# Pooled attention and two feed-forward layers in one kernel: conversions in equal pieces, attention stages at fixed slots, batch 0's value sums issued first

## The chip, the cores and the metric

The kernel runs on one core of a Trainium2 chip. A core has five engines that each work through a queue of their own, in order: PE (matrix products), DVE (elementwise work and reductions), ACT (copies and functions), POOL and SP (here mostly issuers of DMAs). They wait for each other by semaphores. The metric is the time of one execution in microseconds on the device; lower is better.

## The reference, cut to what matters

```python
# q, k, v: (8 batches, 8 heads, 576 positions, 64); keys and values are averaged over groups of 8 positions (72 left)
scores = scale * np.matmul(q, k_p.transpose(0, 1, 3, 2))
attn = softmax(scores)                       # over 72
x = np.matmul(attn, v_p)                     # -> (4608 tokens, 512)
x = (((x @ w1) * (x @ w2)) @ w3) @ w_out     # d_ff 1024
h = x @ w_in                                 # d_ff 2048
out = (softplus(h)) @ w_out2
```

Everything is float32, and the weights of the linear layers arrive as 64-bit words, which the kernel converts.

## The kernel before, in words

**Tiling.** The 4608 tokens are 6 passes (s = 0 to 5) of 768 tokens. Attention works on 36 groups (g) of 128 tokens, six for a pass, one pass ahead of its use. Each float32 product is three fast products of a high and a low part: `split` (L126) makes the parts, a copy on ACT (L128) and a subtraction on DVE (L129); `mm3` (L131) issues the three (L133 to L135). The first layer's `w3 @ w_out` is multiplied into one matrix W beforehand ("the fold", `W_mm`, L552).

**Stages in time.** First the fold, with groups 0 to 2 beside it. Then pass 0 with plain products, 16 `plain_step`s (L685). Then passes 1 to 5, each 8 `one_step`s (L739) of seven products (a Strassen scheme that needs sums of quarters of the weights and of x); their result x2 goes to DRAM. Then the second layer (from L894), 48 steps that reload x2, multiply by `w_in`, apply softplus and multiply by `w_out2`.

**Slots.** Between the products of a step the code calls a slot: four in a plain step, seven in `one_step`. Each slot may issue products of the x2 accumulation (`x2_groups`), one or more stages of attention (`att_slot`, from the table `sched` that `stages` and `begin` fill, L484 to L502), a part of the next pass's x factors (`x_steps`, L656) and a number of steps of background work (`bg`, L214). All of this is written out in program order; nothing is reordered later, so what a slot issues stands in each engine's queue at that place.

**Attention of a group.** `scores` (PE, L405), `maxima` (DVE, L417 and L418), `exps` (ACT, L424, one for each head), `normalize` (DVE, L429 to L431), `p_transpose` (PE L440 and a copy on ACT, L441), `pv` (PE, L456). Keys and values are summed over eight positions by DMAs that accumulate into one buffer (`pool_step`, L369): each waits for the one before on POOL's queue. Batch 0's keys are summed on DVE instead (`pool_k0`, L362), its values by two chains of four DMAs (L377) and one addition on DVE (L380).

**Background.** `next_job` (L199) converts the weights in pieces: `magnitudes` on ACT (L148), then pieces on DVE (L157 and L159, L162, L167), for w12 also a split (L172, L176). After these jobs `left_factors` (L256) runs through the rest of the program: sums of the quarters of w12 (8 tiles), conversion and sums of `w_in` (8 tiles, raw load L265), conversion of `w_out2` (8 tiles, raw load L338, pieces L244 to L251, copies L329, differences L331). Its results go to DRAM from a ring of two staging buffers (`put`, L275: copy L279, difference L281, DMA L285) and come back as weights by `load_factors` on POOL's queue (L637). `load_x2` (L795) reloads x2 for the second layer on SP's queue, first at the end of step 5 of pass 5.

Of the kernel before, what the change touches and what calls it, by code (L numbers as in the profile page):

```python
# [51 lines left out]
def pooled_attention_two_ffn(ctx: ExitStack, tc: tile.TileContext, qT_d, k0_d, kT_d, v_d, w12_d, w3T_d, wo_d, wi_d, wo2_d, out):  # L52
# [98 lines left out]
    def convert_steps(raws, dsts, y, ahead):  # L151
# [11 lines left out]
        yield  # L163
# [5 lines left out]
        if isinstance(dsts[0], tuple):  # L169
            yield  # L170
# [71 lines left out]
    def convert_1024(raw, y):  # L242
        yi = y.bitcast(I32)
        nc.scalar.activation(y, raw[:, :, 1].bitcast(F32), AF.Abs, scale=HI_SCALE)  # L244
        yield
        nc.vector.tensor_scalar(y, y, HI_MIN, HI_MAX, op0=ALU.max, op1=ALU.min)
        nc.vector.tensor_scalar(yi, yi, 3, None, op0=ALU.logical_shift_left)
        yield
        nc.vector.scalar_tensor_tensor(yi, raw[:, :, 1], -0x80000000, yi, op0=ALU.bitwise_and, op1=ALU.bitwise_or)
        yield  # L250
        nc.vector.scalar_tensor_tensor(yi, raw[:, :, 0], 29, yi, op0=ALU.logical_shift_right, op1=ALU.bitwise_or)  # L251
        yield

    sums_made = set()

    def left_factors():  # L256
# [4 lines left out]
        a11, a12, a22, a21 = (y[:, 256 * i:256 * i + 256] for i in range(4))  # L261
# [5 lines left out]
        def sums():  # L267
            nc.vector.tensor_add(s1, a21, a22)
            nc.vector.tensor_sub(s3, a11, a21)
            yield  # L270
            nc.vector.tensor_sub(s2, s1, a11)
            nc.vector.tensor_sub(s4, a12, s2)
            yield

        def put(src, dsts):  # L275
            n = src.shape[1]
            st = stage([P, 2, 512])[:, :, :n]
            hi = st[:, 0, :].bitcast(F32R)
            nc.scalar.activation(hi, src, AF.Copy)  # L279
            yield  # L280
            nc.vector.tensor_sub(st[:, 1, :].bitcast(F32R), src, st[:, 0, :])  # L281
            n //= len(dsts)
            for i, dst in enumerate(dsts):
                dst = dst.rearrange("p h c f -> p h (c f)") if len(dst.shape) == 4 else dst
                nc.sync.dma_start(dst, st[:, :, n * i:n * i + n])  # L285
            yield

        def put_sums(w3_, w4_):
            yield from put(S[:, :512], [w3_[:, :, 2, :], w4_[:, :, 0, :]])
            yield from put(S[:, 512:], [w4_[:, :, 1, :], w4_[:, :, 3, :]])  # L290
# [7 lines left out]
        for t in range(F8):  # L298
            y = ys[t % 2]
            a11, a12, a22, a21 = (y[:, 256 * i:256 * i + 256] for i in range(4))  # L300
            if t + 1 < F8:
                nc.sync.dma_start(ys[(t + 1) % 2], w12y[t + 1])
            yield from sums()
# [704 lines left out]
```

## Time and profile before

| what | value |
|---|---|
| median of 3 runs | 1601.32 us (1600.45 to 1604.28) |
| the profiled execution | 1600.07 us |
| its span on the core | 1598.2 us |
| PE busy | 1507.9 us (94%) |
| DVE, ACT, POOL busy | 1056.2, 838.1, 225.4 us |
| DMA over the span | 311.84 MB, mean 195 GB/s |

The span is the stretch that the trace covers. Rows of the view by windows give, for a stretch of the span in us, each engine's busy time with the number of its instructions in brackets, the mean granted clock of PE (1.00 is 2.4 GHz, 0.50 is 1.2 GHz), the busy share of the DMA engines and what they moved. Rows of the waits name who waited for whose instruction and line, in us over all, the number of waits, and the longest. Rows of a timeline give start, duration, engine, line, operation, output<-input with sizes and the count of merged instructions, and in brackets the engine's idle time just before, with what ended it. Rows of the groups by line give the total and the mean in ns of one. DMA rows give the count, the size of one, and the median from issue to landing in us. Lines are those of the kernel before.

### The profile page before, as it was taken

The numbers are of one execution on the slowest core, as the hardware profiler recorded it, in microseconds if no ns is written. First come the engines' busy times: TensorE is split into PE (matmuls) and PEld (weight loads), VectorE is DVE, ScalarE is ACT, GpSimd is POOL, SyncE is SP. The second block draws the span as 40 slices with busy tenths as digits, with TensorE's granted clock in tenths as the row PEclk, the third lists the DMA queues.
The fourth block names the chain that finished last, engine by engine and source line by source line (L and its number), as shares of the span: only waits on it lengthen the run. The fifth ranks groups of instructions, "written<-read, shape, count | busy, mean of one in ns | idle before, by whom it ended". The sixth has DMA issues, their size and how long they took to land.

```text
span 1598.2 us, 22189 instructions
## 1 busy us (share of the span) xinstructions
PE 1507.9 (94%) x8336; PEld 1363.0 (85%) x8336; DVE 1056.2 (66%) x1678; ACT 838.1 (52%) x1780; POOL 225.4 (14%) x347
## 2 busy tenths in 40 slices
PE   3888998989999999999989999999999999999998
PEld 1458998878999999999879988988898998898897
DVE  5777456557566575576536777777677677768665
ACT  3445545445545555553326466556556556556554
POOL 4311221132213131000101100000000000000000
PEclk9899999999999999999999999999999999999999
DMA  8888796788869787768955635336335334434431
GB/s 262 225 268 237 198 265 186 236 238 260 261 216 279 238 239 246 220 224 301 320 195 191 230 119 192 123 113 209 115 120 183 127 119 152 158 113 134 144 111 40
DMA packets 108011, 311.84 MB, mean 195 GB/s; under 512 B 10853, under 2 KB 49893, under 8 KB 95616
## 3 DMA queue, kind: packets, MB, share of 16 engines
q0 software_dynamic: 41296, 189.03, 39.6%
q1 hardware_dynamic: 66608, 121.39, 22.2%
q8 instruction: 66, 1.08, 0.3%
q14 instruction: 41, 0.34, 0.1%
HBM read 249.56 MB, written 60.82 MB: 194 GB/s over the span
## 4 chain that ended last, share of the span: by engine, by line
PE 78%; DVE 10%; DMA 6%; ACT 4%; issue 2%; POOL 0%; SPq 0%; ACTq 0%; DVEq 0%; POOLq 0%
PE o L875 8%; PE o L874 8%; PE o L873 8%; PE X L133 7%; PE X L134 6%; PE X L135 6%; PE Z L133 5%; PE Z L134 5%; PE Z L135 5%; PE x2p L134 3%; PE x2p L133 3%; PE x2p L135 3%; PE pv L456 2%; PE Wp L555 2%; PE sc L405 2%
## 5 line engine op out<-in xcount | busy, mean ns | idle before, releaser
L133 PE MATMUL X<-area_r 128*128 128x384 f32 x528 | 182.8, 346 | 9.9 <-DVE area_f L768 7.8
L134 PE MATMUL X<-area_r 128*128 128x384 f32 x528 | 178.0, 337 | 0.0
L135 PE MATMUL X<-area_r 128*128 128x384 f32 x528 | 177.8, 337 | 0.0
L128 ACT ACTIVATE area_r<-area_f 128x768 fp32r<-128x768 f32 (+1 forms) x153 | 108.7, 723 | 127.4 <-DVE area_f L775 88.0
L129 DVE TENSOR_TENSOR area_r<-area_f,area_r 128x768 fp32r<-128x768 f32 (+1 forms) x153 | 121.9, 807 | 81.0 <-ACT area_r L128 80.7
L642 POOL DMA_DIRECT2D area_r<-wis x96 | 51.0, 531 | 696.8 <-PE X L135 684.8
L845 ACT ACTIVATE area_f<-area_f 128x768 f32<-128x768 f32 x96 | 81.3, 847 | 126.8 <-DVE area_f L939 125.3
L875 PE MATMUL o<-area_w,area_r 128*128 128x512 f32 x360 | 142.6, 396 | 0.3 <-DVE area_r L129 0.3
L874 PE MATMUL o<-area_w,area_r 128*128 128x512 f32 x360 | 141.9, 394 | 0.0
L873 PE MATMUL o<-area_w,area_r 128*128 128x512 f32 x360 | 140.0, 389 | 0.0
L133 PE MATMUL Z<-area_r 128*128 128x384 f32 x384 | 131.4, 342 | 8.2 <-DVE area_f L759 8.2
L849 DVE TENSOR_SCALAR area_f<-area_f 128x768 f32<-128x768 f32 x96 | 53.8, 561 | 122.0 <-ACT area_f L846 122.0
L134 PE MATMUL Z<-area_r 128*128 128x384 f32 x384 | 129.2, 337 | 0.0
L135 PE MATMUL Z<-area_r 128*128 128x384 f32 x384 | 128.8, 336 | 0.0
L133 PEld LDWEIGHTS X<-area_r 128*128 128x128 f32 x528 | 99.8, 189 | 21.2 <-DVE area_f L768 11.1
L424 ACT ACTIVATE pr<-sc,mx 128x72 f32<-128x72 f32 x288 | 88.5, 330 | 37.4 <-DVE mx L418 36.6
L134 PEld LDWEIGHTS X<-area_r 128*128 128x128 f32 x528 | 99.9, 189 | 3.9
L642 POOL DMA_DIRECT2D area_r<-w12s x80 | 46.9, 587 | 387.9 <-PE X L135 369.9
L135 PEld LDWEIGHTS X<-area_r 128*128 128x128 f32 x528 | 99.7, 189 | 0.0
L855 DVE TENSOR_TENSOR area_f<-area_f 128x768 f32<-128x768 f32 x96 | 92.0, 958 | 6.7 <-ACT area_f L852 0.5
L851 DVE SCALAR_TENSOR_TENSOR area_f<-area_f 128x768 f32<-128x768 f32 x96 | 92.0, 958 | 3.2
L854 DVE SCALAR_TENSOR_TENSOR area_f<-area_f 128x768 f32<-128x768 f32 x96 | 91.4, 952 | 0.0
(166 smaller groups left out, 3895.6 us busy)
## 6 DMA issues: line engine op xcount, KB each, us to landing
area_r<-wis POOLq DMA_DIRECT2D x48, 1024.0 KB, 5.1
area_r<-w12s POOLq DMA_DIRECT2D x40, 1024.0 KB, 6.2
area_r<-wis POOLq DMA_DIRECT2D x48, 768.0 KB, 4.5
area_r<-w12s POOLq DMA_DIRECT2D x40, 768.0 KB, 6.5
area_f<-in_wo_dram SPq DMA_DIRECT2D x24, 512.0 KB, 5.0
wis<-area_f SPq DMA_DIRECT2D x40, 256.0 KB, 5.5
vb<-in_v_dram POOLq DMA_DIRECT2D x64, 144.0 KB, 5.6
xr<-x2d SPq DMA_DIRECT2D x12, 768.0 KB, 7.6
```

The lines of the kernel that those rows point to most:

```text
L128: nc.scalar.activation(hi, src, AF.Copy)
L129: nc.vector.tensor_sub(lo, src, hi.bitcast(F32))
L133: nc.tensor.matmul(ps, whi, xhi, start=first, stop=False, skip_group_check=resumed)
L134: nc.tensor.matmul(ps, whi, xlo, start=False, stop=False, skip_group_check=resumed)
L135: nc.tensor.matmul(ps, wlo, xhi, start=False, stop=last, skip_group_check=resumed)
L642: nc.gpsimd.dma_start(wgroup[n, i], src[i].bitcast(F32R))
L851: nc.vector.scalar_tensor_tensor(e, u, 1.0, e, op0=ALU.subtract, op1=ALU.subtract)
L854: nc.vector.scalar_tensor_tensor(c, c, 0.0, e, op0=ALU.max, op1=ALU.subtract)
L855: nc.vector.tensor_add(c, c, u)
L873: nc.tensor.matmul(oacc[s][i], hl[:, 0, ts], wh, start=first, stop=False)
L874: nc.tensor.matmul(oacc[s][i], hl[:, 0, ts], wl, start=False, stop=False)
L875: nc.tensor.matmul(oacc[s][i], hl[:, 1, ts], wh, start=False, stop=last)
```

## The change

The conversions' generators yield less often, so that one background step holds a piece of work of about equal size: the empty steps are gone, `left_factors` no longer goes through `put` but issues two copies in one step (`highs`) and the two differences with their DMAs in another (`lows`), and `sums` is one step. A job of the fold takes 3 steps instead of 4, a job of w12 4 instead of 6, and `left_factors` 156 instead of 235. The counts of steps in each slot are new. Attention groups begin at other slots, and from group 12 on each group lies at the same seven slots of a step: scores in slot 3, four exps in slot 4 and four in slot 5, normalize in slot 6, the transposition in slot 1 of the next step and pv in its slot 2. Background steps then run in slots 0, 2 and 4 of steps 0 to 5 of passes 1 to 4, in five slots of other steps, and hardly beside the x factors, of which one piece goes into each slot of the last step and the first slots of the next; before pass 1 two go into each of four slots. Batch 0's value sums are issued earlier on POOL's queue. What is computed is the same; only the order of the instructions changes.

```diff
         for i in both:
             nc.vector.scalar_tensor_tensor(yi[i], raws[i][:, :, 1], -0x80000000, yi[i], op0=ALU.bitwise_and, op1=ALU.bitwise_or)
-        yield
         ahead()
         yield
...
         yield
         if isinstance(dsts[0], tuple):
-            yield
             for i in both:
...
-        def put(src, dsts):
-            n = src.shape[1]
-            st = stage([P, 2, 512])[:, :, :n]
-            hi = st[:, 0, :].bitcast(F32R)
-            nc.scalar.activation(hi, src, AF.Copy)
-            yield
-            nc.vector.tensor_sub(st[:, 1, :].bitcast(F32R), src, st[:, 0, :])
...
+        def highs(*srcs):
+            for src in srcs:
+                st = stage([P, 2, 512])[:, :, :src.shape[1]]
+                nc.scalar.activation(st[:, 0, :].bitcast(F32R), src, AF.Copy)
+                staged.append((src, st))
+
+        def lows(*dsts):
+            for to in dsts:
+                src, st = staged.pop(0)
+                nc.vector.tensor_sub(st[:, 1, :].bitcast(F32R), src, st[:, 0, :])
+                n = src.shape[1] // len(to)
+                for i, dst in enumerate(to):
+                    dst = dst.rearrange("p h c f -> p h (c f)") if len(dst.shape) == 4 else dst
+                    nc.sync.dma_start(dst, st[:, :, n * i:n * i + n])
...
         for t in range(F8):
-            yield from convert_1024(raw, y)
+            magnitude()
+            yield
+            shift()
+            yield
+            sign()
+            if t:
+                highs(S[:, :512], S[:, 512:])
+            yield
+            tail_of(t - 1)
+            yield
+            last_bits()
             if t + 1 < F8:
                 load_wi(t + 1)
             else:
                 load_raw_wo2(raw, 0)
-            yield from sums()
+            yield
+            sums(y)
+            yield
+            highs(y[:, :512], y[:, 512:768])
+            yield
             w3_, w4_ = wis[t]
-            yield from put(y[:, :512], [w3_[:, :, 0:2, :]])
-            yield from put(y[:, 512:768], [w4_[:, :, 2, :]])
-            yield from put_sums(w3_, w4_)
+            lows([w3_[:, :, 0:2, :]], [w4_[:, :, 2, :]])
+            yield
...
-    begin = [6 * n for n in range(3)] + [START + 1 + 13 * n // 2 for n in range(9)]
-    begin += [PLAIN + STEADY * s + 1 + 8 * n for s in range(4) for n in range(6)]
+    begin = [6 * n for n in range(3)] + [START + 2 + 19 * n // 3 for n in range(9)]
+    begin += [PLAIN + STEADY * s + 7 * n + 3 for s in range(4) for n in range(6)]
...
-        return [(0, all_[0]), (0, all_[1]), (1, es(0, 1)), (2, es(2, 3, 4)), (3, es(5, 6, 7)), (4, tail[0]), (6, tail[1]), (7, tail[2])]
+        return [(0, all_[0]), (0, all_[1]), (1, es(0, 1, 2, 3)), (2, es(4, 5, 6, 7)), (3, tail[0]), (5, tail[1]), (6, tail[2])]
...
         load_q(0)
+        kv_step()
         make_identity(nc, ident)
...
         for n in range(NJ0):
-            bg(4)
+            bg(3)
             for m in ((0, 1), (2,), (3,), ())[n]:
                 pool_k0(m)
-            if n:
-                kv_step()
+            kv_step()
             W_ready(6)
...
-        for slot in (0, 2, 4):
-            at(slot, kv_step)
+        at(3, kv_step)
         for n in range(START):
             att_slot()
             W_ready(2)
-            bg((1, 2, 2)[n % 3])
+            bg((1, 1, 2)[n % 3])
...
                 att_slot()
-                bg(2 if half == 0 and n < 4 else 1)
+                bg(1)
...
-                if (half, n) == (1, F8 - 1):
+                if (half, n) == (1, F8 - 1) and slot_now[0] > PLAIN - 4:
+                    next(xs)
                     next(xs)
...
+            tile = s < NS - 1 and n < 6
+            steps = (2, 4) if n == 0 else () if n == 7 else (0, 2, 4) if tile else (0, 3, 4, 5, 6)
+
             def slot(k):
-                x2_groups((1, 0, 1, 0, 1, 1, 4)[k])
-                busy = slot_now[0] in heavy
+                x2_groups(((1, 0, 0, 0, 1, 2, 4) if tile else (1, 1, 1, 0, 1, 1, 3))[k])
                 att_slot()
-                if n in (0, F8 - 1) and next(xs_of[s + (n > 0)], True) is None and k % 3:
-                    return
-                if not busy and k != 5:
-                    bg(2 if s == NS - 1 and k in (3, 6) else 1)
+                if n in (0, F8 - 1):
+                    next(xs_of[s + (n > 0)], None)
+                if k in steps:
+                    bg(1)
```

The first place is POOL's queue at the start of the program, before group 0's `pv`. `vb_0`, `vb_1` are the buffers of batch 0's values, `kT` the pooled keys that the scores read. Before:

```order
L358 DMA area_f<-in_k_dram 128x576 x4
L350 DMA q_143<-in_qT_dram 128x512
masks.py:197 MEMSET ident 128x128
masks.py:199 ISA
masks.py:199 AFFINE_SELECT ident<-ident 128x128
L533 MEMSET kT_134 128x576
L533 MEMSET kT_135 128x576
L367 COPY kT_134<-area_e 64x72 x6
L377 DMA vb_0_197<-in_v_dram 72x512
L377 DMA vb_1_198<-in_v_dram 72x512
L367 COPY kT_134<-area_e 64x72 x2
```

The same queue after the change, from its first load of the values:

```order
L405 DMA vb_0_145<-in_v_dram 72x512
L405 DMA vb_1_146<-in_v_dram 72x512
masks.py:197 MEMSET ident 128x128
masks.py:199 ISA
masks.py:199 AFFINE_SELECT ident<-ident 128x128
L561 MEMSET kT_134 128x576
L561 MEMSET kT_135 128x576
L395 COPY kT_134<-area_e 64x72 x4
L405 DMA vb_0_145<-in_v_dram 72x512
L405 DMA vb_1_146<-in_v_dram 72x512
L395 COPY kT_134<-area_e 64x72 x2
L405 DMA vb_0_145<-in_v_dram 72x512
```

The first pair of value loads moved ahead of eight copies and memsets, and the other pairs stand between the copies instead of behind six of them.

The second place is SP's queue at the end of pass 5. `w2s` are the converted tiles of `w_out2` on their way to DRAM, `area_f<-in_wo_dram` a raw load of it, `x2d_69` the x2 of pass 0 that the second layer's first factors are made from. Before:

```order
L338 DMA area_f<-in_wo_dram 128x1024 x2
L332 DMA w2s_121<-area_f 256x1x512 x2
L332 DMA w2s_122<-area_f 256x1x512
L798 DMA xr_127<-x2d_69 128x4x384
L798 DMA xr_128<-x2d_69 128x4x384
L332 DMA w2s_122<-area_f 256x1x512
```

After:

```order
L366 DMA area_f<-in_wo_dram 128x1024 x2
L274 DMA w2s_121<-area_f 256x1x512 x2
L642 DMA x2d_73<-area_e 128x384 x3
L274 DMA w2s_122<-area_f 256x1x512 x2
L642 DMA x2d_73<-area_e 128x384
L826 DMA xr_127<-x2d_69 128x4x384
L826 DMA xr_128<-x2d_69 128x4x384
```

The reload no longer stands between two stores of the last `w_out2` tile; that tile is finished before it, and the last raw load lies further ahead.

The third place is ACT's queue around group 16's transposition in pass 1. L279 and, after the change, L264 are copies into a staging buffer that must have been stored before; L441 and L469 bring the transposed probabilities to `pv`. Before:

```order
L279 ACTIVATE area_f<-area_f 128x512
L424 ACTIVATE pr_2602,sm_2604<-sc_1_2595,mx_2603 128x72 x3
L762 ACTIVATE area_f<-X 128x384
L765 ACTIVATE area_f<-Z 128x384
L279 ACTIVATE area_f<-area_f 128x512
L441 ACTIVATE pT_2688<-pTp_0_2689 72x512
L441 ACTIVATE pT_2688<-pTp_1_2695 72x512
```

After:

```order
L264 ACTIVATE area_f<-area_f 128x512 x2
L793 ACTIVATE area_f<-Z 128x384
L452 ACTIVATE pr_2609,sm_2611<-sc_0_2601,mx_2610 128x72 x4
L452 ACTIVATE pr_2609,sm_2611<-sc_1_2602,mx_2610 128x72 x4
L128 ACTIVATE area_r<-area_f 128x384 x2
L784 ACTIVATE area_f<-X 128x384
L469 ACTIVATE pT_2691<-pTp_0_2692 72x512
L469 ACTIVATE pT_2691<-pTp_1_2698 72x512
```

The staging copy no longer stands right ahead of the transposition's copies; both of a pair come together, some six slots earlier.

## Rows read from the trace of the kernel before

**Rows 1.** Busy time by windows, seven stretches of the span.

```profile
core 0: us, PE busy (x) PEld busy (x) DVE busy (x) ACT busy (x) POOL busy (x), PEclk, DMA share, GB/s
...
40.00:60.00 20.00, 15.63 (x68) 9.27 (x68) 14.67 (x32) 6.44 (x23) 6.02 (x8) 0.74 0.79 207
...
80.00:103.70 23.70, 22.29 (x53) 9.50 (x51) 16.17 (x32) 8.87 (x15) 4.47 (x7) 1.00 0.99 325
...
103.70:250.70 147.00, 132.27 (x885) 125.11 (x885) 90.42 (x194) 75.99 (x248) 27.70 (x35) 0.98 0.77 221
250.70:366.00 115.30, 101.95 (x639) 92.82 (x639) 70.99 (x133) 56.46 (x175) 26.64 (x38) 0.96 0.76 224
366.00:475.00 109.00, 108.15 (x726) 104.26 (x726) 65.38 (x127) 59.72 (x182) 24.42 (x35) 1.00 0.83 254
...
703.00:818.00 115.00, 98.74 (x531) 95.74 (x532) 69.37 (x107) 40.90 (x74) 11.69 (x22) 0.96 0.85 293
900.00:1000.00 100.00, 100.00 (x497) 89.43 (x497) 73.12 (x96) 60.41 (x86) 6.91 (x13) 1.00 0.44 143
```

**Rows 2.** Waits of PE over the whole span, longest first.

```profile
PE Wp L555 <- DVE fold L167: 17.2, 2, 15.9
PE pv L456 <- DVE vb L380: 13.5, 1, 13.5
PE pTp L440 <- DVE pr L431: 10.6, 7, 3.3
PE Z L133 <- DVE area_f L759: 10.4, 5, 6.5
PE pv L456 <- ACT pT L441: 9.0, 4, 4.2
PE X L133 <- DVE area_f L768: 7.8, 9, 1.3
...
PE Z L133 <- ACT area_f L765: 4.2, 2, 2.3
```

**Rows 3.** Timeline of POOL in the first 60 us.

```profile
21.21 2.32 POOL L377 DMA_DIRECT2D vb<-in_v_dram  x2
...
28.43 1.77 POOL L377 DMA_DIRECT2D vb<-in_v_dram  x2 [4.32 <-DMA vb<-in_v_dram]
...
39.48 0.81 POOL L377 DMA_DIRECT2D vb<-in_v_dram  x1 [0.50 <-DMA vb<-in_v_dram]
```

**Rows 4.** Timeline of DVE during the fold.

```profile
31.71 1.29 DVE L162 SCALAR_TENSOR_TENSOR fold<-area_f,fold 128x512 int32<-128x512 int32 x2
43.39 0.69 DVE L380 TENSOR_TENSOR vb<-vb,vb 72x512 f32<-72x512 f32 x1 [10.39 <-DMA vb<-in_v_dram]
...
102.95 4.87 DVE L129 TENSOR_TENSOR area_w<-Wp,area_w 128x512 fp32r<-128x512 f32 x8 [7.36 <-ACT area_w L128]
```

**Rows 5.** Timeline of PE, end of the fold.

```profile
77.98 24.30 PE L555 MATMUL Wp<-fold 128*128 128x512 f32 x56 [1.27 <-DVE fold L167]
```

**Rows 6.** Timelines of ACT and PE around group 16's pv.

```profile
335.20 0.63 ACT L279 ACTIVATE area_f<-area_f 128x512 fp32r<-128x512 f32 x1 [6.49 <-DMA wis<-area_f]
...
336.37 1.55 PE L456 MATMUL pv<-pT,vb 72*64 72x128 f32 x16 [4.16 <-ACT pT L441]
```

**Rows 7.** Timelines of ACT and SP in pass 5.

```profile
751.77 1.12 ACT L244 ACTIVATE area_f<-area_f 128x1024 f32<-128x1024 f32 x1 [3.30 <-DMA area_f<-in_wo_dram]
...
788.98 1.49 SPq L798 DMA_DIRECT2D xr<-x2d  x2
...
806.82 0.84 ACT L128 ACTIVATE area_r<-xr 128x768 fp32r<-128x768 f32 x1 [6.67 <-DMA xr<-x2d]
```

**Rows 8.** Group by line: an x factor's subtraction.

```profile
L129 DVE TENSOR_TENSOR area_r<-xr,area_r 128x768 fp32r<-128x768 f32 x50 | 47.6, 954 | 24.2 <-ACT area_r L128 23.7
```

**Rows 9.** DMA issues by line: stores from the staging buffers.

```profile
wis<-area_f SPq DMA_DIRECT2D x40, 256.0 KB, 5.5
...
w12s<-area_f SPq DMA_DIRECT2D x32, 256.0 KB, 3.2
```

More of the change, by code (lines that the diff above doesn't have):

```diff
@@ L298, in left_factors @@
         for t in range(F8):
-            y = ys[t % 2]
-            a11, a12, a22, a21 = (y[:, 256 * i:256 * i + 256] for i in range(4))
             if t + 1 < F8:
                 nc.sync.dma_start(ys[(t + 1) % 2], w12y[t + 1])
-            yield from sums()
-            yield from put_sums(*w12s[t])
+            sums(ys[t % 2])
+            yield
+            highs(S[:, :512], S[:, 512:])
+            yield
+            lows(*sum_places(*w12s[t]))
             sums_made.add(t)
-        y = ys[0]
-        a11, a12, a22, a21 = (y[:, 256 * i:256 * i + 256] for i in range(4))
+            yield
+            yield
         load_wi(0)
@@ L316, in left_factors @@
                 load_raw_wo2(raw, 0)
-            yield from sums()
+            yield
+            sums(y)
+            yield
+            highs(y[:, :512], y[:, 512:768])
+            yield
             w3_, w4_ = wis[t]
-            yield from put(y[:, :512], [w3_[:, :, 0:2, :]])
-            yield from put(y[:, 512:768], [w4_[:, :, 2, :]])
-            yield from put_sums(w3_, w4_)
+            lows([w3_[:, :, 0:2, :]], [w4_[:, :, 2, :]])
+            yield
         for t in range(F8):
-            yield from convert_1024(raw, y)
+            magnitude()
+            yield
+            shift()
+            yield
+            sign()
+            if t == 0:
+                highs(S[:, :512], S[:, 512:])
+            yield
+            if t == 0:
+                tail_of(F8 - 1)
+                yield
+            last_bits()
             if t + 1 < F8:
                 load_raw_wo2(raw, t + 1)
-            for i in range(2):
-                src = y[:, 512 * i:512 * i + 512]
-                st = stage([P, 2, 512])
-                nc.scalar.activation(st[:, 0, :].bitcast(F32R), src, AF.Copy)
-                yield
-                nc.vector.tensor_sub(st[:, 1, :].bitcast(F32R), src, st[:, 0, :])
-                nc.sync.dma_start(w2s[t][:, :, i, :], st)
-                yield
+            yield
+            highs(y[:, :512], y[:, 512:])
+            yield
+            lows(*([w2s[t][:, :, i, :]] for i in range(2)))
+            yield
     def load_raw_wo2(raw, t):
@@ L521, in att_slot @@
         return fns
-    heavy = {begin[g] + o for g in range(12, NG) for o in (0, 4)}
     with tc.manual_schedule():
@@ L726, in pooled_attention_two_ffn @@
             plain_step(1, n, slot_plain(1, n))
-        for _ in range(2):
-            next(xs)
+        next(xs)
         while pending:
```

42 lines of the change are left out of this document (19 added, 23 removed).

## The prediction

> **What bounds the kernel now.** I read the windows first, then PE's waits, then for each large wait the timeline of the engine that PE waited for. The windows [rows 1] show three kinds of stretch. From 900 us on PE is busy in all of the 100 us and nothing else is near full: the second layer is bound by PE, and an edit that leaves its matrix products alone wins nothing there. Pass 2 (366 to 475 us) is the same with attention beside it: 0.85 us of its 109.0 us are idle. The other stretches have holes: 147.0 - 132.3 = 14.7 us in the plain pass, 115.3 - 102.0 = 13.3 us in pass 1, 115.0 - 98.7 = 16.3 us in pass 5. Pass 5 is the clearest: it has no attention work at all, and yet it takes 115.0 us against pass 2's 109.0.
>
> The waits of PE [rows 2] say what the holes are. The seven rows hold 72.7 us; 15.9 of them is the start of the program, before the first weights are converted. The rest is of two sorts: one long wait for batch 0's values (13.5 us), and many short ones in which DVE or ACT is late with something small, since something of the background stands ahead of it in that engine's queue. So the change is priced wait by wait, and not by the engines' busy time, which stays the same but for the order.
>
> **Batch 0's values.** POOL issues the first loads of the values at 21.21 us, behind the key copies, the second at 28.43, and the last of the chain at 39.48 [rows 3]; DVE's addition runs at 43.39 after 10.39 us of idleness [rows 4], and PE's 13.5 us hang on it. After the change the first pair is issued before the identity is made and the second behind four copies, so that at the time of the old first pair (21.2 us) the third pair goes out. From the second pair to the last issue two links took 39.48 - 28.43 = 11.05 us, so 5.5 us for one, and the landing 3.9 us: the last pair goes out at about 26.7 and lands at about 30.7 us. DVE comes free for the addition at 43.39 - 10.39 = 33.0 us, and since the new order puts the addition ahead of a pair of pieces of 1.29 us [rows 4], at 31.7 us. So the wait for the DMAs goes, and what is late next is DVE's own queue: 43.4 - 31.7 = 11.7 us earlier. From the other side, if each link takes the 7.2 us of the first (28.43 - 21.21), the last pair goes out at 28.4 + 7.2 = 35.6 at the worst, and the gain is about 4 us.
>
> Does that reach the end of the fold? Behind the pv the fold is a chain of DVE's conversions and PE's products, ending in 56 products of 24.3 us that PE runs without a hole after a wait of 1.27 us for DVE [rows 5]; both engines move forward together. Beside those 24.3 us the shorter generators put more on DVE: by the program's order some seven more pairs of pieces, 7 x 1.29 = 9.0 us, before the fold's result is split. DVE was idle for 7.36 us there [rows 4], so 1.6 us stick out. Net 11.7 - 1.6 = 10 us. I take **-10** (from -3 to -12).
>
> **The plain pass and pass 1.** PE waits 7 times for the normalized probabilities, 10.6 us, at most 3.3 [rows 2]. The stages keep their distances in the plain pass (four slots from the scores to the transposition), so the usual wait stays; but in the first four steps a slot held two background pieces in DVE's queue and now holds one. I take the half of it off: **-4** (-8 to +2, since a piece is now larger). PE's waits for the transposed probabilities (9.0 us, four) are a matter of ACT's queue. The longest, 4.16 us, is told by ACT [rows 6]: a staging copy stood 6.49 us in front of its buffer, which a store had not left, with the copies for pv behind it. After the change the staging copies come in pairs, three background steps behind the stores of the same buffers, and in passes 1 to 4 these steps lie two slots or more apart. I take **-7** of the 9.0 (0 to -9).
>
> **The seams and pass 5.** Three rows of [rows 2] remain, 10.4 + 7.8 + 4.2 = 22.4 us. The largest single wait, 6.5 us, is the reload of x2: SP issued it at 788.98 us behind a store of the last `w_out2` tile, and ACT sat 6.67 us in front of it until 806.82 [rows 7], 17.8 us after the issue. In the new order the tile is finished in the middle of step 5 and SP has nothing left to wait for ahead of the reload, so it goes out some four slots earlier, before the loads that POOL issues at the end of the step; 6.5 us can go whole. The waits for ACT's L765 (4.2 us) stand behind a conversion that waits for its raw load (3.30 us at 751.77 [rows 7]); pass 5 now does about four `w_out2` tiles and not eight, with two raw loads in it. The rest, 3.9 us on L759 and 7.8 on L768, lies in the x factors at the passes' ends, where background pieces stood in the same slots and do so no more. Of 22.4 us I leave 6: **-16** (-8 to -20).
>
> **The clock.** A granted clock of 0.74 over 20 us, 0.98 over 147, 0.96 over 115.3 and 0.96 over 115 [rows 1] means 2 x (1 - clock) x length at the lower level of 1.2 GHz: 10.4 + 5.9 + 9.2 + 9.2 = 34.7 us, each beside one of the holes above, against none in 366 to 475 us, which has no hole of note. Half of that time would be saved if PE had been working through all of it, 17 us; part of it was idle and is counted already. I take **-5** (0 to -17).
>
> **What is added.** Ahead of pass 1 two pieces of the x factors go into each slot, and all nine are queued on DVE before the first sum of pass 1, where six were: 3 x 0.95 us [rows 8] = 2.9 us, partly beside PE's first products: **+2** (0 to +4). In pass 1 the x2 products that could stand behind a step's last product are used up before it, so that normalize in slot 6 and the transposition in slot 1 have only about two products between them: six groups, from nothing to the mean of the old waits (10.6 / 7 = 1.5 us) for each: **+2.5** (0 to +9). A few pairs of staging copies lie in consecutive slots (step 6, pass 5) and may meet a store of 5.5 us [rows 9]: **+2** (0 to +8).
>
> **The sum.** -10 - 4 - 7 - 16 - 5 + 6.5 = -35.5 us, from the profiled execution's 1600.07: 1564.6. The median of the runs lies 1.25 us above that execution, so 1565.8; I say 1566 us. The likeliest case's own range is 1550 to 1580.
>
> **A rule that speaks against it.** The Trainium skill, "DMA: Bandwidth & Descriptors", section "Issuing engines are not separate DMA queues", says that DMAs of all issuing engines run on the same 16 DMA engines and interleave, so that issuing early from POOL or SP buys no bandwidth. What it would do here is the first rival, which is worked out from rows alone.
>
> **Rival 1: the DMA engines become the bound of the fold.** From 80 to 103.7 us they are busy for 0.99 of the time at 325 GB/s [rows 1]. A job of w12 reads 1 MB of raw weights and writes 1.25 MB, 2.3 MB or 7 us at that rate, and the new order has one and a half more of them before the end of the fold: 10.5 us, which is all that the values gave. Then the time is 1566 + 10.5 = 1577 us (1570 to 1588). For it: the share of 0.99. Against it: in 40 to 60 us it is 0.79 [rows 1], stores of w12 hold up nobody during the fold, and the loads that the last pieces need are issued three jobs ahead.
>
> **Rival 2: waits only change hands.** PE, DVE and ACT run each step in lockstep, so that a piece taken from one slot is missed in the next, and only the long wait for the values is really gone: 1601.3 - 10 = 1591 us. For it: the short waits have four different releasers. Against it: pass 2, with as much attention and background as its neighbours, has under 1 us of holes.
>
> **Rival 3: slower, by the staging ring.** The pair of copies takes both buffers at once, so the next pair must wait until both stores of the last one have landed, with the exps and the copies for pv behind it on ACT. There are 32 such pairs; the price of one that is late is 4.16 us of PE [rows 6]. It decides where a store takes longer than three background steps: in the plain pass a slot takes 147 / 64 = 2.3 us, so the limit is 6.9 us, against 3.2 us for the stores of w12 and 5.5 for those of `w_in` [rows 9]. Ten late pairs cancel the gain (1566 + 42 = 1608 us); for slower than 1606 us about a third of all must be late. For it: one store did take so long that ACT waited 6.49 us. Against it: the medians.
>
> **How the numbers follow.** Chances: forecast 0.65, rival 1 0.19, rival 2 0.08, rival 3 0.08. The range reaches from the lower end of the forecast's own (1550) to the upper end of rival 1 (1588), and leaves out rival 2, rival 3 and the forecast's tails. A difference of 0.3% (4.8 us) is about what a measurement can tell from no change. Faster by more: the forecast, rival 1 and most of rival 2, 0.88; within: 0.05; slower: rival 3, 0.07.
>
> **What would show it.** The wait of pv on L380 under 2 us, and DVE's addition at 31 to 34 us; the fold's last product before 95 us (with rival 1 after 98, and ACT's conversions waiting for raw loads there). Pass 1 near 110 us, and no wait of pv behind a staging copy; pass 5 under 100 us and no wait on the x2 reload. A clock of 1.00 in pass 1 and pass 5. I would be wrong if staging copies wait for stores in many steps (rival 3), if pass 1 shows a wait for L431 in each step, or if the seam ahead of pass 1 costs more than 5 us.

## The result, and the profile after

The changed kernel takes 1584.33 us (median of 4 runs, 1583.22 to 1590.61) against 1601.97 us for the kernel before on the same chip: a ratio of 0.9897, 95% interval [0.9868, 0.9925]. A second set of runs gave 0.9906 [0.9883, 0.9929]. The gain is 15 to 18 us, where 35 were forecast. The profiled execution took 1584.17 us, its span is 1582.2.

PE's waits over the whole span of the changed kernel, longest first; they answer to [rows 2] (L459 was L431, L802 was L774, L787 was L759, L408 was L380, L796 was L768, L469 was L441):

```profile
PE Wp L583 <- DVE fold L166: 17.3, 2, 15.6
PE pTp L468 <- DVE pr L459: 13.3, 6, 4.6
PE X L133 <- DVE area_f L802: 8.2, 10, 1.5
PE Z L133 <- DVE area_f L787: 4.9, 5, 2.8
PE ab L133 <- DVE area_w L129: 4.4, 1, 4.4
PE pv L484 <- DVE vb L408: 4.3, 1, 4.3
PE X L133 <- DVE area_f L796: 4.0, 5, 1.2
PE pv L484 <- ACT pT L469: 3.3, 4, 1.4
```

Most of the waits that were to go did go: the values from 13.5 to 4.3, L787 from 10.4 to 4.9, L796 from 7.8 to 4.0, the transposed probabilities from 9.0 to 3.3, ACT's late Z sum (4.2) entirely. The wait for the normalized probabilities, which was to lose 4 us, grew from 10.6 to 13.3, and the wait of the first product behind the fold (`ab`) grew to 4.4. Its row in the kernel before, which [rows 2] leaves out:

```profile
PE ab L133 <- DVE area_w L129: 1.4, 1, 1.4
```

Where that is shows best by stage. For all kernels of this study the stages are cut at the same marks: the first product behind the fold, and in passes 1 to 5 ACT's copy of X after the third product of the pass's first step (for pass 5 also of its last). So "plain" below holds the plain pass and the seam into pass 1. Windows at these marks (fold, plain, pass 1, pass 5), first of the kernel before, then of the changed kernel:

```profile
0.00:103.70 103.70, 69.97 (x225) 34.58 (x225) 71.46 (x150) 37.82 (x97) 34.08 (x48) 0.92 0.86 262
103.70:258.25 154.55, 138.62 (x906) 131.21 (x907) 97.90 (x205) 79.79 (x254) 27.70 (x35) 0.96 0.74 213
258.25:371.49 113.24, 100.83 (x650) 91.65 (x650) 68.28 (x130) 56.86 (x177) 26.64 (x38) 0.98 0.79 235
...
711.11:807.56 96.45, 83.78 (x463) 81.31 (x462) 55.96 (x88) 33.31 (x62) 11.16 (x21) 0.98 0.91 313
```

```profile
0.00:99.54 99.54, 72.04 (x224) 35.36 (x225) 79.78 (x168) 42.69 (x107) 31.23 (x48) 0.95 0.93 291
99.54:258.99 159.45, 139.40 (x897) 131.24 (x897) 94.59 (x197) 79.08 (x251) 27.97 (x35) 0.95 0.75 217
258.99:374.05 115.06, 103.41 (x648) 93.64 (x648) 72.13 (x137) 59.89 (x180) 27.06 (x40) 0.95 0.81 245
...
715.14:796.23 81.09, 80.35 (x464) 79.95 (x463) 43.58 (x73) 26.71 (x53) 10.62 (x20) 1.00 0.90 311
```

The same marks in one profiled execution of each kernel, in us (the last columns are medians of all runs and the ratio to the kernel before on the same chip, with its interval). The profiled execution lies within 3 us of its kernel's median, but for three: with the early reload and with the fold's end it was the fastest of six and 4 us under the median, with six steps, seam and fold's end 4 us over it.

| kernel | fold | plain | pass 1 | 2 to 4 | pass 5 and behind | median | ratio |
|---|---|---|---|---|---|---|---|
| before | 103.7 | 154.6 | 113.2 | 339.6 | 887.0 | 1601.97 | 1 |
| changed | 99.5 | 159.4 | 115.1 | 341.1 | 867.1 | 1584.33 | 0.9897 [0.9868, 0.9925] |
| changed, again | 98.7 | 161.6 | 114.8 | 341.0 | 867.5 | 1585.84 | 0.9906 [0.9883, 0.9929] |
| before + values first | 98.2 | 153.5 | 114.6 | 339.4 | 889.3 | 1594.60 | 0.9957 [0.9942, 0.9972] |
| changed, values back | 106.5 | 160.6 | 114.9 | 341.2 | 867.3 | 1591.99 | 0.9937 [0.9920, 0.9954] |
| before + early reload | 105.5 | 153.5 | 108.2 | 340.0 | 877.3 | 1590.32 | 0.9923 [0.9905, 0.9941] |
| before + reload, moved steps | 104.6 | 153.5 | 114.7 | 358.4 | 869.8 | 1602.68 | 1.0006 [0.9993, 1.0019] |
| before + w12 sums in pairs | 103.9 | 170.0 | 106.0 | 338.6 | 871.4 | 1593.27 | 0.9957 [0.9936, 0.9977] |
| changed + third buffer | 97.8 | 160.1 | 114.9 | 341.6 | 867.2 | 1583.73 | 0.9887 [0.9870, 0.9905] |
| changed + six steps a tile | 99.3 | 148.7 | 109.6 | 339.7 | 869.7 | 1570.19 | 0.9811 [0.9787, 0.9835] |
| changed + five steps a tile | 97.9 | 150.0 | 112.2 | 340.4 | 866.3 | 1568.61 | 0.9793 [0.9778, 0.9808] |
| changed + seam | 99.0 | 158.4 | 114.0 | 341.3 | 868.3 | 1582.96 | 0.9883 [0.9861, 0.9904] |
| changed + fold's end | 97.2 | 154.9 | 111.9 | 339.4 | 868.8 | 1578.04 | 0.9855 [0.9830, 0.9879] |
| six steps + seam + fold's end | 96.3 | 142.9 | 111.3 | 340.6 | 885.7 | 1574.82 | 0.9832 [0.9813, 0.9851] |
| five steps + fold's end | 96.4 | 149.4 | 112.3 | 340.0 | 865.8 | 1567.97 | 0.9800 [0.9782, 0.9819] |
| five steps + seam + fold's end | 97.5 | 141.6 | 111.8 | 340.3 | 865.6 | 1560.51 | 0.9749 [0.9728, 0.9771] |

The first two rows say it: the change won 19.9 us in pass 5 and just behind it and 4.2 in the fold, and lost 4.8 in the plain pass, 1.9 in pass 1 and 1.5 in passes 2 to 4. Everything from the end of the fold to the end of pass 1 was forecast to gain. In pass 1 it is not more waiting: PE's idle time there went from 12.4 to 11.7 us, and its busy time from 100.8 to 103.4, at a granted clock of 0.95 and not 0.98.

### The profile page after: what moved, and what is told of

It is laid out like the page before. It is cut to its first block, busy times and chain, and to the rows that moved or that the text cites. A ratio compares the mean times of both kernels' runs of the same rounds, so it can differ in the third digit from the quotient of the medians.

```text
span 1582.2 us, 22215 instructions
## 1 busy us (share of the span) xinstructions
PE 1510.2 (95%) x8336; PEld 1363.3 (86%) x8336; DVE 1052.3 (67%) x1678; ACT 841.1 (53%) x1780; POOL 220.8 (14%) x347
## 4 chain that ended last, share of the span: by engine, by line
PE 78%; DVE 7%; ACT 4%; DMA 3%; issue 1%; SPq 1%; ACTq 0%; DVEq 0%
PE o L903 8%; PE o L902 8%; PE o L901 8%; PE X L133 7%; PE X L134 7%; PE X L135 7%; PE Z L133 6%; PE Z L134 5%; PE Z L135 5%; PE x2p L134 3%; PE x2p L135 3%; PE x2p L133 3%; PE pv L484 2%; PE sc L433 2%; PE pTp L468 2%; DVE area_r L129 1%
## 5 line engine op out<-in xcount | busy, mean ns | idle before, releaser
L668 POOL DMA_DIRECT2D area_r<-w12s x80 | 43.7, 547 | 439.8 <-PE X L135 411.8
```

The costliest lines, as they stand in the source:

```text
L668: nc.gpsimd.dma_start(wgroup[n, i], src[i].bitcast(F32R))
```

## The experiments

**What the values are worth.** The kernel before with this part alone, and the changed kernel without it:

```
         load_q(0)
+        kv_step()
         make_identity(nc, ident)
...
-            if n:
-                kv_step()
+            kv_step()
...
-        for slot in (0, 2, 4):
-            at(slot, kv_step)
+        at(3, kv_step)
```

> The kernel before, with only batch 0's value sums issued first. In the changed kernel the wait of pv for the addition fell from 13.5 to 4.3 us, but the fold's end moved by 4.2 us only. Theory A (the waits behind it gave 4 us back, since the generators in equal pieces stand ahead of W's split): here, with the old pieces, DVE still has idle time ahead of the split, so the whole 8 us arrive: 1594 us (1592 to 1596), the first product after the fold near 95.5 us. Theory B (the DMA engines bound the fold: raw loads of w12 come late whatever is done): 3 to 5 us arrive, 1597 us.

> The changed kernel, with batch 0's value sums at their old places in POOL's queue. Theory A: the wait of pv is back near 13 us, and since W's split was late by 3 us of DVE's work anyway, 4 to 6 us of it show: 1589 us. Theory B (the end of the fold is bound by DMAs): 0 to 3 us, 1586. If the forecast's term of 10 us held in full: 1594.

By itself the part gave 0.43%, 7 us; the fold ended 5.5 us earlier in the profiled execution. Taken out of the changed kernel it cost 5 to 6 us (0.9937 against 0.9897 and 0.9906, with intervals that overlap), and the fold of the profiled execution ended 7 to 8 us later. In the kernel before theory A holds, and neither theory B nor 10 us. In the changed kernel the cost is there, but the runs do not tell 5 us from 3 or from 8. Why DVE's addition came 8.2 us earlier (43.39 [rows 4] to 35.20) and not 11.7 is told by POOL and DVE of the changed kernel:

```profile
15.40 0.90 POOL L405 DMA_DIRECT2D vb<-in_v_dram  x1 [3.13 <-DMA vb<-in_v_dram]
...
22.50 0.82 POOL L405 DMA_DIRECT2D vb<-in_v_dram  x1 [4.13 <-DMA vb<-in_v_dram]
...
29.26 1.67 POOL L405 DMA_DIRECT2D vb<-in_v_dram  x2 [4.08 <-DMA vb<-in_v_dram]
...
35.20 0.69 DVE L408 TENSOR_TENSOR vb<-vb,vb 72x512 f32<-72x512 f32 x1 [2.35 <-DMA vb<-in_v_dram]
```

A link of the chain takes 7.1 and 6.8 us (15.40, 22.50, 29.26). The last pair of loads goes out at 29.26 us, and DVE waits 2.35 us for it, until 35.20: what is late is still the chain of DMAs and not DVE's own queue.

**What the end of the fold lost.** PE's wait for the split of W grew from 1.4 to 4.4 us. ACT, then DVE, of the changed kernel there:

```profile
93.80 0.70 ACT L148 ACTIVATE area_f<-area_f 128x512 f32<-128x512 f32 x1 [3.12 <-DMA area_f<-in_w_dram]
```

```profile
96.25 1.29 DVE L174 TENSOR_TENSOR area_r<-area_f,area_r 128x512 fp32r<-128x512 f32 x2 [1.01 <-ACT area_r L170]
97.46 0.75 DVE L157 TENSOR_SCALAR area_f<-area_f 128x512 f32<-128x512 f32 x2
98.13 0.76 DVE L159 TENSOR_SCALAR area_f<-area_f 128x512 int32<-128x512 int32 x2
98.80 4.87 DVE L129 TENSOR_TENSOR area_w<-Wp,area_w 128x512 fp32r<-128x512 f32 x8
```

The raw weights came 3.1 us late, so pieces that should have been done stood ahead of the split at 98.80; in the kernel before DVE was idle there [rows 4]. This has the marks of rival 1, at a third of its size. The edit that takes the pieces out:

```
-                bg((1, 0, 1)[n % 3])
+                bg((1, 0, 1)[n % 3] if len(products) > 8 else 0)
```

> The changed kernel, with no background piece beside the last eight products of the fold. PE waits 4.4 us for DVE's split of W there, behind pieces that waited 3.1 us for raw loads. Theory A (those pieces are the delay, and they fit in later): the wait falls to 1.5 us, 3 us less, 1581. Theory B (what is not done there is late in the plain pass): 0, 1584.

The wait went to 1.4 us and the fold ended 1.5 to 2.4 us earlier, but the median fell by 8 us, most of it (in a profile of the fastest execution) in the plain pass:

```profile
97.17:252.02 154.85, 134.56 (x897) 126.54 (x897) 100.51 (x208) 82.69 (x258) 28.34 (x35) 0.98 0.78 228
```

That was in neither theory. PE is idle there for as long as in the changed kernel (20.3 and 20.1 us); what is shorter is its busy time, 134.6 and not 139.4 us, at a clock of 0.98 and not 0.95. The pieces taken out put all later background off by some steps, so that it meets the attention's stages in other slots; that this is the cause was not tried by itself. With the plain pass mended (five steps a tile, below) the same edit gave 1567.97 us against 1568.61, nothing that can be told apart (0.9800 and 0.9793 of the kernel before). There no more than the 1 to 2 us of the fold can be seen.

**What the plain pass lost.** The longest of PE's waits of the changed kernel behind the start is there. Rows of PE, DVE, ACT and SP (SP's rows give the time of issue):

```profile
204.74 1.59 PE L468 MATMUL pTp<-ident,pr 128*72 128x128 f32 x8 [4.59 <-DVE pr L459]
```

```profile
196.69 0.42 DVE L254 TENSOR_TENSOR area_f<-area_f 128x256 f32<-128x256 f32 x1 [6.98 <-DMA area_f<-w12y]
```

```profile
198.66 0.63 ACT L264 ACTIVATE area_f<-area_f 128x512 fp32r<-128x512 f32 x1 [5.20 <-DVE mx L445]
...
220.02 1.38 ACT L264 ACTIVATE area_f<-area_f 128x512 fp32r<-128x512 f32 x2 [3.57 <-DMA w12s<-area_f]
```

```profile
182.01 2.63 SPq L274 DMA_DIRECT2D w12s<-area_f  x4
184.73 2.08 SPq L642 DMA_DIRECT2D x2d<-area_e  x4
186.86 0.50 SPq L291 DMA_DIRECT2D area_f<-w12y  x1
189.17 3.27 SPq L274 DMA_DIRECT2D w12s<-area_f  x4
```

DVE waited 6.98 us for quarters of w12 that were read back from DRAM, with the maxima of a group behind it; ACT's exps, the normalization and PE's transposition followed in a chain. That load was issued at 186.86 us, behind four stores from the staging buffers and four of x2, and landed 9.7 us later. The next four stores, from 189.17 on, landed only at 198.0 to 199.5 us, so the staging copy at 198.66 would have been late there even with the quarters in time. Further on ACT waits for staging buffers by itself, 7.7 us in four waits, with exps behind it. Is it the load, or the ring? With a third buffer each tile is loaded two ahead:

```
-        ys = [y, mem("f", RAW, [P, 1024])]
+        ys = [y, mem("f", RAW, [P, 1024]), mem("f", RAW + 4, [P, 1024])]
...
-                nc.sync.dma_start(ys[(t + 1) % 2], w12y[t + 1])
+                nc.sync.dma_start(ys[(t + 2) % 3], w12y[t + 2])
```

> The changed kernel, with a third buffer for the quarters of w12, so that each is loaded two tiles ahead. In the plain pass DVE waits 7.0 us for such a load with the maxima of a group behind it, and PE then 4.6 us for that group's probabilities, with the clock at 0.66 after it. Theory A: that wait goes, and 1.7 us of clock with it: the plain pass from 153.8 to 148 us, 1578 us in all. Theory B (the staging ring is the bound there: four waits of ACT of 7.7 us for stores): the steps run into the stores sooner, 0 to 2 us, 1583.

The load's wait was gone, and at the same place ACT now waited for the stores, with PE behind it (rows of ACT and PE):

```profile
196.80 0.63 ACT L264 ACTIVATE area_f<-area_f 128x512 fp32r<-128x512 f32 x1 [4.66 <-DMA w12s<-area_f]
```

```profile
203.11 1.39 PE L469 MATMUL pTp<-ident,pr 128*72 128x128 f32 x8 [4.28 <-DVE pr L460]
```

Waits for staging buffers rose to 14.1 us, the plain stage stayed (160.1). Theory B: taking away one of the two does nothing. So both were relaxed together, by giving a tile its old six steps, and then five (`range(3)`, and `s in (3, 4)`, since fewer steps are added):

```
             lows(*sum_places(*w12s[t]))
             sums_made.add(t)
-            yield
-            yield
+            for _ in range(4):
+                yield
...
-            steps = (2, 4) if n == 0 else () if n == 7 else (0, 2, 4) if tile else (0, 3, 4, 5, 6)
+            steps = (2, 4) if n == 0 else () if n == 7 else (0, 2, 4, 6) if tile and s in (2, 3, 4) else (0, 2, 4) if tile else (0, 3, 4, 5, 6)
```

> The changed kernel, with six steps for each tile of the sums of w12 instead of four, as the kernel before had (the 16 steps more lie in slot 6 of passes 2 to 4). With a third buffer the wait of 7.0 us for the quarters was gone and one of 4.7 us for the stores stood in its place. Theory A (both are one thing: a tile is stored and loaded in four slots of 2.3 us, and the DMAs want longer): both waits go, the plain pass falls from 159 to 152 us or less, 1577 us. Theory B (the short waits in the plain pass come from the attention chain itself, a slot too short): 1 to 2 us, 1583.

> The changed kernel, with five steps for a tile of the sums of w12. Six gave 15 us. Theory A (a limit: stores and load need some 7 to 9 us, and with five steps the pair has four slots or 9.2 us): nearly all of it, 1572 us, waits of the staging copies for stores under 3 us in all. Theory C (each step more gives its share, the load on DVE and ACT in the plain pass counts): half of it, 1578.

Six steps gave 1570 and five 1569 us, 15 to 18 us less than the changed kernel. ACT's waits for the stores in the plain stage, of the changed kernel, with the third buffer, with the fold's end, and with five steps; with six there is no such row:

```profile
ACT area_f L264 <- DMA w12s<-area_f: 7.7, 4, 3.6
ACT area_f L264 <- DMA w12s<-area_f: 14.1, 7, 4.7
ACT area_f L264 <- DMA w12s<-area_f: 15.5, 5, 6.3
ACT area_f L264 <- DMA w12s<-area_f: 6.6, 3, 5.2
```

With five steps one long wait is left (5.2 of 6.6 us, where theory A allowed 3 in all), and the time is the same as with six. As to the time that is theory A's limit and not theory C's share for each step. But the sum of these waits does not order the kernels: with the fold's end it is 15.5 us, and the stage is shorter than in the changed kernel. So a wait of ACT for a store has no fixed price in PE's time. How much of the 15 to 18 us is the limit, and how much a shift of the background against the attention as with the fold's end, is not shown.

One rival can be put aside: more steps a tile also take work of DVE out of the plain stage (94.59 us busy in the changed kernel, 92.23 with five steps, 90.00 with six). In the kernel with five steps and the fold's end, further below, DVE is busy for more than in the changed kernel and the stage is still 10 us shorter. Its window, behind that with five steps alone:

```profile
97.94:247.92 149.98, 136.11 (x897) 128.04 (x897) 92.23 (x192) 77.89 (x250) 27.68 (x35) 0.97 0.79 229
96.42:245.79 149.37, 135.36 (x897) 126.26 (x897) 97.84 (x202) 81.39 (x257) 28.14 (x35) 0.96 0.77 223
```

The cross-check puts the four steps, alone, into the kernel before:

```
-            yield from sums()
-            yield from put_sums(*w12s[t])
+            for _ in sums():
+                pass
+            yield
+            sts = [stage([P, 2, 512]) for _ in range(2)]
+            for i, st in enumerate(sts):
+                nc.scalar.activation(st[:, 0, :].bitcast(F32R), S[:, 512 * i:512 * i + 512], AF.Copy)
+            yield
...
+                nc.vector.tensor_sub(st[:, 1, :].bitcast(F32R), S[:, 512 * i:512 * i + 512], st[:, 0, :])
...
+                    nc.sync.dma_start(dst, st[:, :, 256 * j:256 * j + 256])
+            sums_made.add(t)
+            yield
+            yield
```

> The kernel before, with one part of the change alone: a tile of the sums of w12 in four steps, its copies and stores in pairs, as in the changed kernel. Theory A (this cadence is what costs the plain pass its gain: four stores take 2.6 us to issue and 4.2 to land, against three slots of 2.3 us): slower, the plain pass with its seam from 154.6 to 160 us or more, 1607 us. Theory B (the cadence costs only together with the new attention slots or the fold that ends earlier): no change, 1601 (1598 to 1604).

ACT's waits for staging buffers in its plain pass (none in the kernel before):

```profile
ACT area_f L308 <- DMA w12s<-area_f: 17.3, 6, 5.1
```

The plain stage grew by 15.4 us, to 170.0: the cadence alone is enough for that, without the new slots and without the earlier fold. (It also brings later work into the stage: DVE is busy for 104.6 us there, 97.9 before.) As to the total theory A was wrong by 14 us: the kernel was faster, 1593 us. Its background has 16 steps fewer and ends earlier: pass 5 and what is behind it fell from 887.0 to 871.4, and pass 1 from 113.2 to 106.0.

**What pass 5 won.** The kernel before with the reload of x2 at the end of step 4 of pass 5, not 5:

```
+                if s == NS - 1 and n == 4:
+                    load_x2(0)
                 if s == NS - 1 and n == 5:
...
-                    load_x2(0)
                     load_wo2(0)
```

> The kernel before, with the reload of x2 issued one step earlier in pass 5 and nothing else. Pass 5 fell from 113.8 to 94.1 us by the whole change. Theory A (a sum of separate waits, the reload's 6.5 us the largest, with some clock lost behind it): 6.5 to 9 us less, 1594 us, pass 5 near 106. Theory B (waits change hands: the next x factor is late for its background pieces): 0 to 3 us, 1600.

Pass 5 and behind fell by 9.7 us, the median by 12. (This execution was also 5 us shorter in pass 1, which the edit does not touch: there a wait for a store was shorter.) Theory A, and somewhat more than it said. What is left to the changed kernel's 867.1 us is 10 us, and these are not got by moving conversions:

```
-                    bg(2 if s == NS - 1 and k in (3, 6) else 1)
+                    bg(2 if s == NS - 1 and k in (3, 6) or s in (2, 3, 4) and k == 3 else 1)
```

> The kernel before with the reload of x2 a step earlier (12 us by itself), and with two background steps instead of one in slot 3 of passes 2 to 4, so that pass 5 has fewer conversions of w_out2. Pass 5 was then still 91 us between the marks where the changed kernel has 81, with 8.1 us of PE's idle time. Theory A (what is left in pass 5 are conversions that wait for their raw loads, with the step's own work behind them): 5 to 10 us less than with the reload alone, 1583 us, pass 5 at 82 to 86. Theory B (the conversions only move, and passes 2 to 4 pay): 1590.

Pass 5 and behind came to 869.8 us as theory A has it, but passes 2 to 4 paid 18.4 us against the early reload alone, and the median of 1602.68 us is above theory B's too. In the old form a step more in slot 3 stands ahead of the step's sums; that this is what costs was not tried. In the changed kernel the same is nearly free (1.5 us in passes 2 to 4). The likely reason is that there are fewer steps in all (156, not 235): the cross-check, with 16 fewer, won most of it in pass 5 and paid nothing in passes 2 to 4. The new slots were not tried by themselves.

**The seam ahead of pass 1.** PE of the changed kernel, and the windows of 5 us behind these waits:

```profile
253.34 0.44 PE L134 MATMUL Z<-area_x,area_r 128*128 128x384 f32 x1 [1.68 <-DVE area_x L129]
256.66 0.69 PE L133 MATMUL X<-area_r 128*128 128x384 f32 x1 [2.16 <-ACT area_f L784]
261.75 0.69 PE L133 MATMUL Z<-area_r 128*128 128x384 f32 x1 [2.80 <-DVE area_f L787]
```

```profile
255.00:260.00 5.00, 2.29 (x6) 1.78 (x6) 4.97 (x9) 3.00 (x7) 0.64 (x2) 0.63 0.70 221
260.00:265.00 5.00, 3.25 (x11) 3.25 (x12) 1.69 (x3) 0.79 (x2) 1.70 (x2) 0.50 0.88 239
```

DVE is busy for 4.97 of the first 5 us: it works off the queued pieces of the x factors and four sums of a background step (257.08 to 258.54 us), and the sum on L787, which PE waits for, comes last. One piece a slot, from slot 76 on:

```
-                if (half, n) == (1, F8 - 1) and slot_now[0] > PLAIN - 4:
-                    next(xs)
+                if half and slot_now[0] > PLAIN - 7:
                     next(xs)
...
-        next(xs)
         while pending:
```

> The changed kernel, with the x factors of pass 1 at one piece a slot over the last seven slots of the plain pass and the first two of pass 1, instead of two a slot over four. At that seam PE now waits 1.7 + 2.2 + 2.8 = 6.6 us and the clock is at 0.63, 0.50 and 0.85 in the three stretches of 5 us from 255 us on. Theory A (the nine pieces queued on DVE ahead of the first sum of pass 1 are the cause): 4 to 7 us less, 1578 us. Theory B (PE has no x2 products to go on with at that seam, whatever the order): 0 to 2 us, 1583.

3 us at most against the changed kernel as it is (0.9883 and 0.9906, with intervals that overlap): nearer to theory B, by itself.

**All together.** The first expectation is of the kernel with six steps, the second of that with five, the third of five without the seam's edit.

> The changed kernel with six steps for a tile of the sums of w12 (15 us by itself), the fold's end free of background pieces (8 us by itself) and the x factors at one piece a slot ahead of pass 1 (3 us by itself). If the three are independent: 1559 us. If the fold's end gave its 8 us mainly by shifting the background against the attention in the plain pass, which six steps do already: 1566 us.

> The changed kernel with five steps a tile, the fold's end free of pieces, one x piece a slot ahead of pass 1, and the background's extra steps in slot 6 of passes 2 to 4, so that it ends no later than with five steps alone. With six steps the three together took fold, plain pass and seam from 258 to 239 us, but pass 5 and the second layer were 18 us longer, since the reload of x2 went out 15 us later, behind the last store of w_out2. Theory A (the only thing in the way is that the background ends too late): both halves hold, 1558 us (1553 to 1563), pass 5 at 81 us and 786 behind it. Theory B (the pieces taken out of the fold's end are missed in every stage after it): 1570.

> The same without the edit of the x factors: five steps a tile and the fold's end free of pieces. If the seam ahead of pass 1 is worth the 3 us it gave by itself: 1561 us where the other is 1558. If it gave nothing but a shift: the same as the other.

With six steps the time was 1574.82 us, neither 1559 nor 1566: fold and plain came to 239.2 us (258.9 in the changed kernel), but 18.6 us were lost in pass 5 and behind it. SP and DVE of that kernel show the old wait again:

```profile
744.78 20.43 SPq L274 DMA_DIRECT2D w2s<-area_f  x4
765.26 1.46 SPq L824 DMA_DIRECT2D xr<-x2d  x2
```

```profile
790.12 0.96 DVE L687 TENSOR_TENSOR xr<-xr,xr 128x768 f32<-128x768 f32 x1 [7.01 <-DMA xr<-x2d]
```

The background ended too late, so the reload went out behind the last stores, 74 us into pass 5 (765.26 against the pass's mark at 691.0), where the changed kernel has it at 51 us. With five steps and room in slot 6 the reload goes out at 50 us, and all of it holds: 1560.51 us, a ratio of 0.9749 [0.9728, 0.9771], the best of the study and 2.5% under the kernel before. Theory A. The seam, 3 us by itself, is worth 7.5 us here (1567.97 to 1560.51), with the plain stage at 141.6 and not 149.4 us and at a clock of 1.00 and not 0.96; why it is worth more here was not tried. The windows of this best kernel for fold, plain, pass 1 and pass 5:

```profile
0.00:97.55 97.55, 71.66 (x225) 35.31 (x225) 72.55 (x152) 37.69 (x97) 31.38 (x48) 0.95 0.92 287
97.55:239.10 141.55, 132.13 (x897) 124.60 (x897) 95.65 (x199) 81.50 (x256) 27.92 (x35) 1.00 0.78 229
239.10:350.90 111.80, 101.44 (x648) 91.44 (x648) 67.66 (x132) 56.07 (x175) 27.34 (x40) 0.98 0.80 238
691.11:771.15 80.04, 80.04 (x464) 79.98 (x463) 42.23 (x71) 26.53 (x52) 10.59 (x20) 1.00 0.87 302
```

## Why the forecast was half right

**The step that failed: the plain pass and pass 1.** The -7 for the transposed probabilities came nearly true at PE (9.0 to 3.3 us). The -4 for the normalized ones went the other way (10.6 to 13.3), and the plain stage grew by 4.8 us. The working had the staging copies "three background steps behind the stores of the same buffers" and put the stores at nothing there; rival 3 set 6.9 us for three slots against "3.2 us for the stores of w12". That compares the landing of one store with what a pair of buffers waits for: one DVE subtraction, then four issues in a row on SP, 2.5 to 3.5 us for the four, and the landing of the last. The landing itself was longer, too (stores of the changed kernel, 150 to 250 us):

```profile
DMA to landing us min/median/max: 2.5/4.2/8.9
```

From the first issue of a tile's four stores to the last landing, the eight tiles of the changed kernel took 7.3, 5.4, 4.8, 10.4, 5.4, 8.7, 7.6 and 7.1 us: five of eight are over the 6.9. With five steps two of eight are over the 9.2 us of four slots, with six none is over the 11.5 of five (10.0 at most). And the load of the next quarters is issued behind these stores, and takes 7.0 us (its median there). The working looked at the staging ring and not at the load that runs at the same pace. So rival 3's mechanism was right, with 8 tiles where it decides (the sums of w12) and not 32 pairs; its place in the argument, a case of its own at 0.08, was wrong: it holds beside the gains of the forecast, not in place of them. The edit that gives a tile more steps is worth 15 to 18 us, of a miss of 18 to 20.

Stage by stage, the profiled executions differ by -15.9 us where -35.5 were forecast: -4.2 in the fold (forecast -10), +8.2 from there to the end of pass 4 (-4.5, with what was added), -19.9 in pass 5 and behind it (-16), and the -5 for the clock went to no stage. With five steps it is -5.8, -4.8 and -20.7. That this kernel, at 1569 us, ends near the forecast's 1566 is partly luck: too much was forecast for the fold and the clock, too little for pass 5.

**The values** (-10): right in kind, worth 5 to 7 us. The link of 5.5 us was too short, 6.8 to 7.1 was measured; so was the landing of 3.9 us, with 5.9 from the last issue to DVE's addition. And DVE's own queue was not what came next. The working's other side, with links of 7.2 us, counted one link too many: from the third pair at 21.2 us one link leads to a last issue at 28.4 (29.26 was measured), and 35.6 us is then about where it lands, a gain near 8 us and not 4. The 1.6 us that were to stick out at the fold's end became 3.0, by late raw weights: the end that rival 1 names. The Trainium skill, "DMA: Bandwidth & Descriptors", section "Issuing engines are not separate DMA queues", says that DMAs of all issuing engines run on the same 16 DMA engines and interleave. The trace agrees with this much: in the fold these engines were busy for 0.93 of the time (0.86 before) and moved 291 GB/s, and ACT waited 3.12 us for weights there. That the share is what made the weights late was not tried.

**Seams and pass 5** (-16): right; 19.9 us with the clock that came back, pass 5 at 81 us and at a clock of 1.00. Half is the reload (9.7 us alone). The rest goes with the smaller number of steps: the cross-check, with 16 fewer and no edit of the reload, has 15.6 of the 19.9.

**The clock** (-5): next to nothing. 2 x (1 - clock) x length gives the time at 1.2 GHz, to the rounding of the clock: before 16.6 + 12.4 + 4.5 + 3.9 = 37.4 us in fold, plain, pass 1 and pass 5, after 10.0 + 15.9 + 11.5 + 0 = 37.4. It left pass 5 and the fold, and came back beside the new waits. Over the whole span the mean granted clock went from 0.986 to 0.988, some 45 to 38 us at the lower level, which is worth some 3 us. In the best kernel it is 9.8 + 0 + 4.5 + 0 = 14.3.

**What was added.** The normalization in pass 1 (+2.5) cost nothing: no wait for L459 behind 236 us. Staging in passes 1 to 5 (+2): one wait of 3.5 us on ACT, none on PE. The seam (+2) cost 3 to 7.5 us, and PE's three waits there hold 6.6: it was named as what would prove the forecast wrong above 5.

## What to carry to other kernels

When steps are merged so that fewer slots do the same work, buffers that go through DRAM come round sooner: for each such ring add up the issue time of every transfer ahead on the queue, the landing and the read, and compare that with the slots until its next use. When a wait for a load vanishes and a wait for a store stands in the same place, as with the third buffer, suspect the pace of both before either buffer. And a schedule's end is a term of its own: a saving early on moves the last background step, and what is queued behind it, against the work that needs it.

## What was not expected of the hardware

Issuing was not small beside moving: four stores of 256 KB stood 2.5 to 3.5 us in SP's queue of the changed kernel, and one landed in 4.2 us (median). Pairs of reloads of 768 KB landed in 7.6 us in the median of the kernel before; the first pair, beside other loads and stores, took 17.8 and 22.5 us there, and 15.5 and 23.9 in the kernel with six steps, seam and fold's end. And one late store of pass 1 held ACT up by 6.5, 6.3, 6.2 and 3.0 us in four kernels that share this stretch of code word for word (the kernel before, with values first, with reload and moved steps, with the early reload), and pass 1 took 113.2, 114.6, 114.7 and 108.2 us: a term built on one such wait (the 4.16 us of [rows 6]) should carry that spread.
